# A linear attention and a gated feed-forward on one core: tile 1's first layer as products of quarters, w_in used and summed by column groups, and the loads around it in another order

## The chip, the cores and the metric

The kernel runs on one core of a Trainium2 chip, in one launch. The time is device microseconds of that core. Lower is better.

## The reference, cut to what matters

```python
# batch 8, heads 8, seq 576, head_dim 64;  d_model 512 = 8 x 64, d_ff 2048; all float32
kv  = einsum('bhsd,bhse->bhde', k, v)
out = einsum('bhsd,bhde->bhse', q, kv)
rms = sqrt(mean(out * out, axis=-1, keepdims=True) + 1e-6)
x   = (out / rms * g_norm)            # then (B*S, H*D) = (4608, 512)
h   = x @ w_in                        # (4608, 512) x (512, 2048)
g   = h / (1 + exp(-1.702 * h))       # the gate
y   = g @ w_out                       # (4608, 2048) x (2048, 512)
```

## The kernel before

**Tiles.** The 4608 rows are nine tiles of 512 rows. Tile t (0 to 7) holds 512 of batch t's 576 rows; the last 64 rows of all eight batches make tile 8. For each tile there is a first layer (x times w_in, 16 column blocks of 128, each 4 deep in k) with the gate, and a second layer (the gated values times w_out). Between the instructions of tile t's layers stand those of batch t+1's attention, which makes the x of the next tile. Data are float16 in SBUF (the POOL queue's DMAs convert), sums are float32 in PSUM.

**Dense and seven products.** Tile 0 is dense in both layers (`dense(..., deep=True)`): 64 matmuls of 512 columns each. Tiles 2 to 8 use, in both layers, a form of matrix product that splits both operands into quarters and takes seven products of quarters in place of eight, with sums and differences of quarters as operands (`SevenIn` for the first layer, `Seven` for the second). The first layer is done in four parts of two column blocks in the left half and two in the right. A product is two column blocks times two k blocks: 4 matmuls of 256 columns; a part has seven, a tile 28. It needs four sums of w_in's quarters (`ws`, made once by `w_in_sum`), four sums of x's quarters per tile (`Sums.form`), and for each part: a copy of the first product's bank, a copy of the fifth's to SBUF (`s5`), two additions on VectorE (L544, L546), and four gates on ScalarE. The second layer takes differences of w_out (`tw`, by `weight_sum`) and sums of the gated values (`gS`, by `Seven.sums`). Tile 1 is mixed: its second layer is in seven products, its first is dense (`GROUP` and the ordered first columns in `dense`, then L422).

**The weights' scale.** g_norm is folded into w_in for every tile but the first: batch 0's x is multiplied by it directly, so w_in is scaled in place (`scale_w_in`) only after tile 0's first layer has read it. Before, that is done in tile 0's second layer, whole k blocks at a time: two on ScalarE, two on VectorE.

**What sets the order.** Everything is recorded in program order under a manual schedule; each engine runs its instructions in that order, and semaphores carry the dependencies. `u1` and `u2` hold what is put between the steps: `at1(i, f, ...)` behind step i of a tile's first layer, `at2(n, f, ...)` behind matmul n of its second. For tiles in seven products a `Plan` gives the order by hand: `steps` ("21" is part 2's product 1, "kv" the next batch's k-v product), the places of the sums (`ready`, `later`, `xsums`), the engine of each copy (`snap`: D is VectorE, A is ScalarE), the PSUM pools (a, h, o with 3, 3 and 2 banks), and the places of the attention's steps (`attn`).

**Loads.** They go out on the POOL queue in program order, and a load's issue waits for the landing of an earlier one. The order before is: batch 0's q, k, v by pairs of heads with w_in's first four column blocks between; w_in 4-5, 6-7, 8-9, 10-12, 13-15; w_out 0-3; batch 1's q; w_out 4-7; k of pairs 0-1; w_out 8-9, 10-11; v of pairs 0-1; k, then v of pairs 2-3; w_out 12-13, 14-15; batch 2's q; then batch 2's k and v, each whole. The DMA transposes (q of a batch, and its x) and the stores go out on SyncE's queue.

**PE's order around the change.** Tile 0's first layer takes column blocks 0 to 5 as a group, then 6 to 15 one by one; its second layer has 64 matmuls (L760), between which batch 1's q is transposed (L403), its k-v product made (L221, four pairs), its product with q (L254) and its sums of squares (L329). ACT makes the squares and the roots, DVE multiplies (`apply`), which gives tile 1's x.

Of the kernel before, what the change touches and what calls it, by code (L numbers as in the profile page):

```python
# [16 lines left out]
def kernel(  # L17
# [27 lines left out]
    GROUP = 6  # L45
    assert PE_ * NJ == S and PE_ % 32 == 0
# [59 lines left out]
    def load_kv(b):  # L106
        early_load("k", b, 0, NPAIR)
        early_load("v", b, 0, NPAIR)
# [79 lines left out]
    def scale_w_in(ko, engine):  # L188
        w = w_in_sb[:, ko]
        if engine is nc.scalar:  # L190
            engine.activation(w, w, AFT.Copy, scale=g_col)
        else:
            engine.tensor_scalar_mul(w, w, g_col)
# [198 lines left out]
    class Second(Early):  # L392
# [7 lines left out]
        def q(self, c):  # L400
            t = ps_a.tile([P, S], F16, name="q1", tag="att")
            for j in range(NJ):
                nc.tensor.transpose(  # L403
                    t[:, j * PE_ : (j + 1) * PE_],
                    qbuf[0:PE_, (c * NJ + j) * P : (c * NJ + j + 1) * P],
                    ident[0:PE_, 0:PE_],
                )
# [31 lines left out]
    def w_in_sum(n):  # L439

        a11, a12, a21, a22 = quarters(w_in_sb, slice(0, HF * P), slice(0, KH))
        op, a, b = (
            (nc.vector.tensor_add, a21, a22),
            (nc.vector.tensor_sub, ws[:, 0], a11),
            (nc.vector.tensor_sub, a11, a21),
            (nc.vector.tensor_sub, a12, ws[:, 1]),
        )[n]
        op(ws[:, n], a, b)
# [103 lines left out]
    def weight_sum(n):  # L552
        b11, b12 = w_out_sb[:, 0:HF, 0:HN], w_out_sb[:, 0:HF, HN:DM]
        b21, b22 = w_out_sb[:, HF:FO, 0:HN], w_out_sb[:, HF:FO, HN:DM]
        a, b = ((b12, b11), (b22, tw[:, 0]), (b22, b12), (b21, tw[:, 1]))[n]
        nc.vector.tensor_sub(tw[:, n], a, b)

    class Seven:
# [10 lines left out]
        def sums(self, i0, i1, which=(0, 1, 2, 3)):  # L569
            lo, hi = slice(i0, i1), slice(HF + i0, HF + i1)  # L570
            r1, r2 = slice(0, 2 * P), slice(2 * P, SM)
            g, s = self.gT, self.s
            for n in which:
                op, a, b = (
                    (nc.vector.tensor_add, g[:, lo, r2], g[:, hi, r2]),
                    (nc.vector.tensor_sub, s[:, 0, lo], g[:, lo, r1]),
                    (nc.vector.tensor_sub, g[:, lo, r1], g[:, lo, r2]),
                    (nc.vector.tensor_sub, g[:, hi, r1], s[:, 1, lo]),
                )[n]
                op(s[:, n, lo], a, b)  # L580
# [102 lines left out]
    def hid_seven(t, hid, seven, units1):  # L683


        xs = Sums(t, hid.x)
# [7 lines left out]
        for n, step in enumerate(todo.steps):  # L694
# [12 lines left out]
            for i0, i1, which in todo.ready.get(n, ()):  # L707
                seven.sums(i0, i1, (which,))
# [9 lines left out]
        end = lambda: seven.sums(HF - 2, HF, (0,))  # L718
# [6 lines left out]
    def dense(t, units1, units2, group, deep, hid=None):  # L725
        hid = hid or Hidden(t)
        gT = hid.gT
        seven = None if deep else Seven(t, gT)
        cols = range(FO) if deep else [f for i in range(HF) for f in (i, HF + i)]
        ready = {} if deep else {8: (0, 4), 13: (4, 6), 15: (6, 8, (0,))}  # L730
        if group and t:
            order = [(ko, fo) for part in ((0, 3, 1, 2), range(4, group)) for ko in (0, 1) for fo in part]
            order += [(ko, fo) for ko in range(2, KO) for fo in range(group)]
            for ko, i in order:
                pool = (ps_h, "hT") if i < 3 else (ps_a, "att") if i == 3 else (ps_o, "o")
                hid.mm(ko, cols[i], *pool)
            for i in range(group):
                hid.gate(cols[i])
        left = {}
        if t >= SEVEN:  # L740
            left = hid_seven(t, hid, seven, units1)
            cols = ()
        for i, fo in enumerate(cols):
            if i >= group:
# [3 lines left out]
            for u in units1.get(i, ()):  # L748
                u()
            if i in ready:  # L750
                seven.sums(*ready[i])

        osb = osbs[t] = opool.tile([P, 4, DM], F32, name="osb", tag="osb")
        os = {}

        def project(mo, fo):
# [10 lines left out]
            if fo == FO - 1:  # L767
                copy = nc.scalar.copy if mo % 2 else nc.vector.tensor_copy
                copy(osb[:, mo, :], os[mo])

        if deep:
            steps = [(mo, 4 * i + k) for i in range(3) for mo in range(4) for k in range(4)]
            steps += [(mo, f + k) for f in (12, 14) for mo in range(2) for k in range(2)]
            steps += [(mo, 12 + k) for mo in (2, 3) for k in range(4)]
            for n, (mo, fo) in enumerate(steps):
                project(mo, fo)
                for u in units2.get(n, ()):
                    u()
        else:
            later = plan(t).later if t >= SEVEN else {6: ((6, 8, 1),), 30: ((6, 8, 2), (6, 8, 3))}  # L780
            later = {
                n: [lambda x=x: seven.sums(x[0], x[1], (x[2],)) for x in xs] for n, xs in later.items()
            }
            for n, us in units2.items():
                later.setdefault(n, []).extend(us)
            for n, us in left.items():
                later[n] = us + later.get(n, [])
            seven.run(later)
        if t < EARLY:

            n = 0
            while n < SM:
                mo, j, p = n // P, n // PE_, n % PE_
                m = min((mo + 1) * P, (j + 1) * PE_) - n
                nc.sync.dma_start(
                    out=out[t * S : (t + 1) * S, :][bass.DynSlice(NJ * p + j, m, step=NJ), :],
                    in_=osb[n % P : n % P + m, mo, :],
                )
                n += m
        elif t < B and t not in HALVED:  # L800
            store(t, 0, J)
# [70 lines left out]
    for fo in range(4, GROUP):  # L872
        for ko in range(KO - 1):
            d0.mm(ko, fo, ps_o, "o")
    for fo in range(GROUP):
        d0.mm(KO - 1, fo)
    for fo in range(GROUP):
# [11 lines left out]
    load_w_out(14, FO)  # L889

    osbs = {}
    SEVEN = 2
# [26 lines left out]
    FIRST = {  # L919
        "rows": (1, 7, 14, 20),  # L920
        "add_up": (5, 12, 18, 26),
        "table": 21,
        "roots": (32, 32),
        "turn": (33, 34, 35, 36),
    }

    def plan(t):
        return LATER if t < B - 1 else LAST_TWO
# [7 lines left out]
    for t in range(NT):  # L936
# [12 lines left out]
        if t == 0:  # L949
            at1(7, of(0, "out", NPAIR))  # L950
            at2(4, setattr, a0, "ss_pool", Attention.ss_pool)
            at2(4, of(0, "ss", NPAIR, True))
            at2(4, of(0, "apply", NPAIR))
            at1(8, start, 1)
            at2(5, scale_w_in, 0, nc.scalar)
            at2(6, scale_w_in, 1, nc.scalar)
            at2(33, weight_sum, 0)
            at2(33, scale_w_in, 2, nc.vector)
            at2(34, scale_w_in, 3, nc.vector)
            for n, at in ((2, 35), (0, 39), (1, 40)):  # L960
                at2(at, w_in_sum, n)
            for l in range(2):
                at1(9, nc.vector.memset, kvd[l], 0.0)
            at1(13, load_q, 2)
            for c in range(NPAIR):
                at1(12, of(1, "pack_q", c))
                at2(9 + 3 * c, of(1, "q", c))
                at2((36, 37, 46, 47)[c], of(1, "kv", c))
                o = (41, 43, 52, 53)[c]
                at2(o, of(1, "out", c))  # L970
                if c == NPAIR - 1:
                    at2(48, load_kv, 2)
                at2((45, 48, 56, 58)[c], of(1, "ss", c))
                at2((48, 51, 56, 60)[c], of(1, "apply", c))
        elif b < B:
            if t == 1:
                for n in range(1, 4):
                    at1(0, weight_sum, n)
                at1(9, w_in_sum, 3)
            todo = plan(t) if t >= SEVEN else None  # L980
            at1(todo.steps.index("kv") if todo else 11, of(b, "kv_all", todo.keep if todo else "D"))
            late = 15 if todo else 11
            if t == 1:
                at1(5, start, b)
                at1(5, of(b, "transpose_q"))
            if t + 2 < B:
                at1(late, load_kv, t + 2)
# [3 lines left out]
            at = todo.attn if todo else FIRST  # L991
# [18 lines left out]
        dense(t, u1, u2, (GROUP, 5)[t] if t < 2 else 0, t == 0, None if t else d0)  # L1010
# [30 lines left out]
```

## Time and profile before

| what | value |
|---|---|
| median of 3 runs | 264.03 us (263.69 to 264.33) |
| profiled execution: its own time | 263.92 us |
| its span, first to last instruction | 262.1 us |
| granted TensorE clock, mean | 0.996 |
| busy: PE, PEld (weight loads), DVE, ACT, POOL | 253.6, 204.3, 185.1, 173.6, 43.7 us |
| tile 0's first layer, most of it | 16.42 to 28.97 us |
| tile 0's second layer with batch 1's attention | 28.97 to 47.31 us |
| tile 1's first layer | 47.31 to 62.11 us |
| tile 1's second layer | 62.11 to 75.46 us |

Times in the chain of waits are those of the links, which for a run of matmuls begin 0.16 us behind the start of its first one: a matmul of 256 columns is shown with 273 ns, but the next one ends 0.11 us later. In the timeline and in the table of groups the durations are those of single instructions, which on DVE and ACT overlap a little with the next one.

### The profile page before, as it was taken

The numbers are of one execution on the slowest core, as the hardware profiler recorded it, in microseconds if no ns is written. First come the engines' busy times: TensorE is split into PE (matmuls) and PEld (weight loads), VectorE is DVE, ScalarE is ACT, GpSimd is POOL, SyncE is SP. The second block draws the span as 40 slices with busy tenths as digits, with TensorE's granted clock in tenths as the row PEclk, the third lists the DMA queues.
The fourth block names the chain that finished last, engine by engine and source line by source line (L and its number), as shares of the span: only waits on it lengthen the run. The fifth ranks groups of instructions, "written<-read, shape, count | busy, mean of one in ns | idle before, by whom it ended". The sixth has DMA issues, their size and how long they took to land.

```text
span 262.1 us, 6210 instructions
## 1 busy us (share of the span) xinstructions
PE 253.6 (97%) x2556; PEld 204.3 (78%) x2556; DVE 185.1 (71%) x324; ACT 173.6 (66%) x308; POOL 43.7 (17%) x68
## 2 busy tenths in 40 slices
PE   6899999999999999999999999999999999999992
PEld 5434554447888988898889988998899888888882
DVE  1540378868768995899589958995899587567831
ACT  3459836776649963996489748974798469737810
POOL 8863242005005001400050005000000000000000
PEclk9999999999999999999999999999999999999998
DMA  7999999999989946996899769946600620021005
GB/s 173 197 199 205 205 203 177 217 206 130 163 180 172 221 58 160 117 240 83 145 154 196 102 157 150 237 54 154 165 0 8 156 83 0 3 100 63 0 3 160
DMA packets 59806, 35.32 MB, mean 135 GB/s; under 512 B 31554, under 2 KB 57154, under 8 KB 59650
## 3 DMA queue, kind: packets, MB, share of 16 engines
q0 software_dynamic: 28608, 18.17, 50.1%
q1 hardware_dynamic: 30768, 16.36, 27.1%
q8 instruction: 20, 0.33, 0.5%
q10 hardware_dynamic: 402, 0.39, 0.5%
q14 instruction: 8, 0.07, 0.1%
HBM read 36.70 MB, written 9.44 MB: 176 GB/s over the span
## 4 chain that ended last, share of the span: by engine, by line
PE 92%; DMA 4%; POOL 1%; DVE 0%; issue 0%; ACT 0%; ACTq 0%
PE o L648 37%; PE h L530 33%; PE hT L422 10%; PE o L760 5%; PE kvp L221 2%; DMA vbuf<-in_v_dram 2%; DMA qraw<-in_q_dram 2%; PE outR L281 2%; PE ss L329 1%; PE outT L254 0%; PE q L403 0%; PE outT L258 0%; POOL kraw L89 0%; ACT sq L272 0%; DVE osb L628 0%
## 5 line engine op out<-in xcount | busy, mean ns | idle before, releaser
L648 PEld LDWEIGHTS <-gS 128*128 128x128 f16 x512 | 49.8, 98 | 5.5
L510 ACT ACTIVATE gT<-h 128x512 f16<-128x512 f32 x84 | 46.2, 605 | 5.1 <-PE h L530 5.1
L530 PEld LDWEIGHTS <-ws 128*128 128x128 f16 x448 | 43.8, 98 | 5.1
L648 PE MATMUL o<-tw,gS 128*128 128x256 f16 x384 | 46.3, 273 | 0.0
L530 PE MATMUL h<-xS,ws 128*128 128x256 f16 x336 | 45.3, 273 | 0.0
L648 PEld LDWEIGHTS <-gT 128*128 128x128 f16 x384 | 37.1, 98 | 4.2
L530 PEld LDWEIGHTS <-w_in_sb 128*128 128x128 f16 x336 | 32.5, 98 | 3.9
L648 PE MATMUL o<-w_out_sb,gT 128*128 128x256 f16 x256 | 33.3, 273 | 0.0
L422 PE MATMUL hT<-xT,w_in_sb 128*128 128x512 f16 x128 | 28.9, 379 | 0.0
L625 DVE TENSOR_TENSOR osb<-o,qf 128x512 f32<-128x512 f32 (+1 forms) x25 | 16.7, 668 | 15.6 <-PE o L648 12.8
L530 PE MATMUL h<-xT,w_in_sb 128*128 128x256 f16 x192 | 27.1, 273 | 0.0
L89 POOL DMA_DIRECT2D kraw<-in_k_dram x11 | 8.1, 733 | 106.3 <-PE kvp L221 87.8
L580 DVE TENSOR_TENSOR gS<-gT 128x512 f16<-128x512 f16 (+2 forms) x34 | 22.0, 653 | 4.5 <-ACT gT L431 3.9
L544 DVE TENSOR_TENSOR h<-h,s 128x512 f32<-128x512 f32 x28 | 19.5, 698 | 7.4 <-PE h L530 5.6
L422 PEld LDWEIGHTS <-w_in_sb 128*128 128x128 f16 x128 | 12.3, 98 | 15.4 <-issue 0.9
L431 ACT ACTIVATE gT<-hT 128x512 f16<-128x512 f32 x32 | 17.6, 613 | 7.0 <-PE hT L422 7.0
L546 DVE TENSOR_TENSOR s<-h,s 128x512 f32<-128x512 f32 x28 | 19.4, 692 | 4.0 <-PE h L530 3.3
L331 ACT ACTIVATE rs<-ss,eps_t 128x512 f32<-128x512 f32 (+1 forms) x16 | 9.2, 584 | 16.4 <-PE ss L329 16.3
L510 ACT ACTIVATE gT<-s 128x512 f16<-128x512 f32 x28 | 17.3, 628 | 1.2 <-DVE s L546 1.2
L944 ACT ACT_TABLE_LOAD x14 | 18.0, 1283 | 0.3
L681 POOL DMA_DIRECT2D out_dram<-osb x2 | 1.1, 562 | 94.1 <-DVE osb L625 94.1
L760 PE MATMUL o<-w_out_sb,gT 128*128 128x512 f16 x64 | 16.7, 380 | 0.0
(93 smaller groups left out, 367.6 us busy)
## 6 DMA issues: line engine op xcount, KB each, us to landing
out_dram<-osb SPq DMA_DIRECT2D x10, 512.0 KB, 3.5
kraw<-in_k_dram POOLq DMA_DIRECT2D x6, 576.0 KB, 8.7
vbuf<-in_v_dram POOLq DMA_DIRECT2D x6, 576.0 KB, 12.1
qraw<-in_q_dram POOLq DMA_DIRECT2D x3, 512.0 KB, 13.3
qbuf<-in_q_dram POOLq DMA_DIRECT2D x3, 512.0 KB, 14.0
out_dram<-osb SPq DMA_DIRECT2D x6, 192.0 KB, 6.9
w_in_sb<-in_moe_w_in_dram POOLq DMA_DIRECT2D x4, 256.0 KB, 7.5
w_out_sb<-in_moe_w_out_dram POOLq DMA_DIRECT2D x2, 512.0 KB, 14.0
```

Source lines behind the costliest of these rows:

```text
L331: nc.scalar.activation(rs[:, 0:n], t[:, 0:n], AFT.Abs_reciprocal_sqrt, bias=eps_t, scale=1.0 / D)
L422: nc.tensor.matmul(self.h[fo], w_in_sb[:, ko, fo * P : (fo + 1) * P], self.x[:, ko], start=(ko == 0), stop=(ko == KO - 1),)
L431: nc.scalar.activation(self.gT[:, fo, :], self.h[fo], AFT.Gelu_apprx_sigmoid)
L510: nc.scalar.activation(self.gT[:, to, n * TH : (n + 1) * TH], src, AFT.Gelu_apprx_sigmoid)
L530: nc.tensor.matmul(bank[name][:, a], w, x, start=(p in (1, 5) and a == 0 and k == 0), stop=(k == KH - 1), skip_group_check=True,)
L544: nc.vector.tensor_add(bank["z"], bank["x"], self.s5)
L546: nc.vector.tensor_add(self.s5, bank["x"], self.s5)
L580: op(s[:, n, lo], a, b)
L625: nc.vector.tensor_add(o, ps, self.kept[with_][:, m])
L648: nc.tensor.matmul(o, a, w, start=(p in (1, 2, 5) and i == 0 and (mo == 0 or split)), stop=(i == HF - 1), skip_group_check=True,)
L760: nc.tensor.matmul(os[mo], gT[:, fo, mo * P : (mo + 1) * P], w_out_sb[:, fo, :], start=(fo == 0), stop=(fo == FO - 1),)
L944: u2.setdefault(i, []).append(lambda: f(*args))
```

## The change

Five things are done together.

1. Tile 1's first layer becomes 28 products of quarters by a new `Plan`, `SECOND`. Tile 1's x lies as (c, n), so `Sums` takes it without the regrouping; the first sum of x is formed behind step 55 of tile 0's second layer.
2. w_in's column blocks are used by tile 0 in the order `COLS` and loaded in the order 0-3, 8-9, 10-11, 4-7, 12-15. `scale_w_in` and the sums of w_in work on groups of columns (0-3 with 8-11, 4-5 with 12-13, 6-7 with 14-15), all on VectorE: the first two groups between the columns of tile 0's first layer, the third in its second layer.
3. The differences of w_out are made in pieces: in tile 0's second layer, the last three (for blocks 6-7) in tile 1's first.
4. w_out 12-13 is loaded ahead of batch 1's k and v of pairs 2-3; the k-v products of these pairs and what follows from them stand one to three steps later in tile 0's second layer.
5. Batch 2's k and v are loaded in halves, behind steps 39 and 51 of that layer; the copies of batch 1's transposed q out of PSUM go from VectorE to ScalarE.

The function `dense` is split into `layers`, `first_columns`, `project_all` and `store_early`, with no other effect on the order.

```diff
+    COLS = (0, 1, 2, 3, 8, 9, 10, 11, 4, 5, 12, 13, 6, 7, 14, 15)
...
-    load_w_in(4, GROUP)
-    load_w_in(GROUP, 8)
     load_w_in(8, 10)
-    load_w_in(10, 13)
-    load_w_in(13, FO)
+    load_w_in(10, 12)
+    load_w_in(4, 8)
+    load_w_in(12, FO)
...
-    def scale_w_in(ko, engine):
-        w = w_in_sb[:, ko]
-        if engine is nc.scalar:
-            engine.activation(w, w, AFT.Copy, scale=g_col)
-        else:
-            engine.tensor_scalar_mul(w, w, g_col)
+    def scale_w_in(i0, i1):
+
+        for i in (i0, HF + i0):
+            w = w_in_sb[:, :, i * P : (i + i1 - i0) * P]
+            nc.vector.tensor_scalar_mul(w, w, g_col)
...
-            nc.vector.tensor_copy(s, t)
+            nc.scalar.copy(s, t)
             self.qT[c] = s
...
+    def w_in_sums(g0, g1):
+
+        f = slice(2 * g0 * P, 2 * g1 * P)
+        a11, a12, a21, a22 = quarters(w_in_sb, f, slice(0, KH))
+        s = [ws[:, n, :, f] for n in range(4)]
+        nc.vector.tensor_add(s[0], a21, a22)
+        nc.vector.tensor_sub(s[1], s[0], a11)
+        nc.vector.tensor_sub(s[2], a11, a21)
+        nc.vector.tensor_sub(s[3], a12, s[1])
...
-            x = x if t < B else x.rearrange("p c (j r) -> p c j r", j=J)
+            x = x if EARLY <= t < B else x.rearrange("p c (j r) -> p c j r", j=J)
...
-    def weight_sum(n):
...
+    def weight_sum(n, i0, i1):
+
+        lo, hi = slice(i0, i1), slice(HF + i0, HF + i1)
...
     early_load("v", 1, 0, 2)
+    load_w_out(12, 14)
     early_load("k", 1, 2, NPAIR)
     early_load("v", 1, 2, NPAIR)
-    load_w_out(12, 14)
     load_w_out(14, FO)
...
+    SECOND = Plan(
+        "01 15 11 05 02 06 21 16 12 07 25 03 26 22 04"
+        " 35 31 27 13 17 36 kv 32 24 23 14 37 33",
+        {24: ((0, 4, 0),), 26: ((0, 4, 1),), 27: ((4, 6, 0),)},
+        {0: ((0, 4, 3),), 4: ((0, 8, 2),), 26: ((4, 8, 1),), 72: ((4, 8, 3),)},
+        {1: 'AAAA', 5: 'DADD'},
+        "D",
+        "aoaa",
+        "ahoh",
+        {5: '34'},
+        (-1, 0, 0, 4),
+        {'rows': (0, 2, 8, 19), 'add_up': (6, 26, 27, 31), 'table': 26, 'roots': (27, 33), 'turn': (40, 50, 51, 52)},
+    )
...
         if t == 0:
+            for l in range(2):
+                at1(6, nc.vector.memset, kvd[l], 0.0)
             at1(7, of(0, "out", NPAIR))
+            at1(7, scale_w_in, 0, 4)
+            at1(7, w_in_sums, 0, 2)
+            at1(8, start, 1)
+            at1(11, scale_w_in, 4, 6)
+            at1(11, w_in_sums, 2, 3)
+            at1(13, load_q, 2)
...
+            at2(18, weight_sum, 0, 0, HF)
+            at2(18, scale_w_in, 6, 8)
+            at2(18, w_in_sums, 3, 4)
             for c in range(NPAIR):
                 at1(12, of(1, "pack_q", c))
                 at2(9 + 3 * c, of(1, "q", c))
-                at2((36, 37, 46, 47)[c], of(1, "kv", c))
-                o = (41, 43, 52, 53)[c]
...
+                at2((36, 37, 49, 50)[c], of(1, "kv", c))
+                at2((41, 43, 54, 55)[c], of(1, "out", c))
+                at2((45, 50, 58, 60)[c], of(1, "ss", c))
+                at2((48, 52, 58, 62)[c], of(1, "apply", c))
+            for n in range(1, 4):
+                at2(19, weight_sum, n, 0, 4)
+                at2(38, weight_sum, n, 4, 6)
+            at2(39, load_kv, 2, 0, 2)
+            at2(51, load_kv, 2, 2, NPAIR)
+
+            def first_sum():
+                made[1] = Sums(1, xT[1])
+                made[1].form(0)
+
+            at2(55, first_sum)
...
             if t == 1:
                 at1(5, start, b)
                 at1(5, of(b, "transpose_q"))
+                at1(4, nc.scalar.preload_act_table_set, "gelu_apprx_sigmoid_and_others")
+                for n, i in ((1, 8), (2, 11), (3, 16)):
+                    at1(i, weight_sum, n, 6, HF)
```

More of the change, by code (lines that the diff above doesn't have):

```diff
@@ L567, in __init__, with sums @@
             self.bank, self.kept = {}, None
-        def sums(self, i0, i1, which=(0, 1, 2, 3)):
+        def sums(self, i0, i1, *which):
             lo, hi = slice(i0, i1), slice(HF + i0, HF + i1)
@@ L707, in hid_seven @@
             for i0, i1, which in todo.ready.get(n, ()):
-                seven.sums(i0, i1, (which,))
+                seven.sums(i0, i1, which)
         for u in gates:
@@ L723, in hid_seven, with layers, first_columns @@
         return left
[L725 to L744, printed above, removed]
+    def layers(t, units1, units2):
+        hid = d0 if t == 0 else Hidden(t)
+        seven = Seven(t, hid.gT) if t else None
+        left = hid_seven(t, hid, seven, units1) if t else first_columns(hid, units1)
+        osbs[t] = opool.tile([P, 4, DM], F32, name="osb", tag="osb")
+        if t:
+            todo = {n: [lambda x=x: seven.sums(*x) for x in xs] for n, xs in plan(t).later.items()}
+            for n, us in units2.items():
+                todo.setdefault(n, []).extend(us)
+            for n, us in left.items():
+                todo[n] = us + todo.get(n, [])
+            seven.run(todo)
+        else:
+            project_all(hid.gT, units2)
+        if t < EARLY:
+            store_early(t)
+        elif t < B and t not in HALVED:
+            store(t, 0, J)
+    def first_columns(hid, units):
+        for i, fo in enumerate(COLS):
+            if i >= GROUP:
                 for ko in range(KO):
@@ L747, in dense, with project_all @@
                 hid.gate(fo)
-            for u in units1.get(i, ()):
+            for u in units.get(i, ()):
                 u()
-            if i in ready:
-                seven.sums(*ready[i])
-        osb = osbs[t] = opool.tile([P, 4, DM], F32, name="osb", tag="osb")
+    def project_all(gT, units):
         os = {}
@@ L768, in project, with store_early @@
                 copy = nc.scalar.copy if mo % 2 else nc.vector.tensor_copy
[L769 to L801, printed above, removed]
+                copy(osbs[0][:, mo, :], os[mo])
+        steps = [(mo, 4 * i + k) for i in range(3) for mo in range(4) for k in range(4)]
+        steps += [(mo, f + k) for f in (12, 14) for mo in range(2) for k in range(2)]
+        steps += [(mo, 12 + k) for mo in (2, 3) for k in range(4)]
+        for n, (mo, fo) in enumerate(steps):
+            project(mo, fo)
+            for u in units.get(n, ()):
+                u()
+    def store_early(t):
+        n = 0
+        while n < SM:
+            mo, j, p = n // P, n // PE_, n % PE_
+            m = min((mo + 1) * P, (j + 1) * PE_) - n
+            nc.sync.dma_start(
+                out=out[t * S : (t + 1) * S, :][bass.DynSlice(NJ * p + j, m, step=NJ), :],
+                in_=osbs[t][n % P : n % P + m, mo, :],
+            )
+            n += m
     def store(t, j0, j1):
@@ L967 @@
                 at2(9 + 3 * c, of(1, "q", c))
-                at2((36, 37, 46, 47)[c], of(1, "kv", c))
-                o = (41, 43, 52, 53)[c]
[L970 to L974, printed above, removed]
-        elif b < B:
[L976 to L982, printed above, removed]
+                at2((36, 37, 49, 50)[c], of(1, "kv", c))
[11 more added lines that the diff above has]
+            at2(55, first_sum)
+        elif b < B:
+            todo = plan(t)
+            at1(todo.steps.index("kv"), of(b, "kv_all", todo.keep))
             if t == 1:
```

61 lines of the change are left out of this document (18 added, 43 removed).

## The prediction

> **What bounds the kernel now.** I read the page first, then the chain of waits in order of time, then PE's own waits.
>
> ```profile
> span 262.1 us, 6210 instructions
> PE 253.6 (97%) x2556; PEld 204.3 (78%) x2556; DVE 185.1 (71%) x324; ACT 173.6 (66%) x308; POOL 43.7 (17%) x68
> PE 92%; DMA 4%; POOL 1%; DVE 0%; issue 0%; ACT 0%; ACTq 0%
> 22.06 6.91 PE hT L422 x32
> ...
> 31.24 0.26 PE q L403 x6
> ...
> 38.10 0.31 PE kvp L221 x12
> ...
> 41.74 0.31 PE kvp L221 x12
> ...
> 47.31 10.36 PE hT L422 x48
> 57.67 0.88 PE kvp L221 x48
> 58.55 3.56 PE hT L422 x16
> ...
> 77.21 11.02 PE h L530 x100
> ...
> PE idle L831 <- DVE one_t L176: 1.3, 1, 1.3
> ...
> PE outT L254 <- DVE kvb L373: 0.4, 1, 0.4
> ```
>
> The chain is PE for 92% of the span, and tile 1's first layer (47.31 to 62.11 us, with batch 2's k-v product inside) is one unbroken run of PE on it. All of PE's waits (five rows, first and last shown) belong to instructions of batch 0's start. So from tile 0 on TensorE is the limit: each PE microsecond that goes away is worth one, and each wait that is put in costs one. The profiled execution took 263.92 us (span 262.1, 1.8 around it); the median of the three runs is 264.03, and I carry differences over to that median. A change of 0.2%, 0.53 us, is about what a measurement of this kernel can tell.
>
> **1. What the products remove from PE.** Tile 1's dense layer is 64 matmuls 512 wide: 10.36 + 3.56 = 13.92 us (0.2175 each). The new one is 28 products of 4 matmuls 256 wide. 11.02/100 = 0.110 us each, so 112 cost 12.34 (0.441 a product). Removed: **1.58 us**. Batch 2's k-v product (0.88) stays. The sum rests on a 256-wide matmul costing half a 512-wide one, which the rows show, 0.110 against 0.2175. The Trainium skill speaks against this (TensorE: Matmul & The Clock Gate, Back-to-back issue gap): in a stream of weight load and matmul pairs it gives about 131 ns for 512 columns and 81 for 128. By it an estimate between the two, 98 ns for 256, would make the layer 11.0 us against 8.4, a loss of 2.6. The trace does not agree; its 216 to 218 ns decide.
>
> **2. w_in in another order: a new wait in tile 0.** POOL's issues wait for earlier loads, so their starts date the landings.
>
> ```profile
> 16.38 0.76 POOL L180 DMA_DIRECT2D w_out_sb<-in_moe_w_out_dram  x1 [0.25 <-DMA w_in_sb<-in_moe_w_in_dram]
> ...
> 19.00 0.70 POOL L180 DMA_DIRECT2D w_out_sb<-in_moe_w_out_dram  x1 [0.35 <-DMA w_in_sb<-in_moe_w_in_dram]
> 20.33 0.72 POOL L180 DMA_DIRECT2D w_out_sb<-in_moe_w_out_dram  x1 [0.62 <-DMA w_in_sb<-in_moe_w_in_dram]
> 22.61 0.69 POOL L89 DMA_DIRECT2D vbuf<-in_v_dram  x1 [1.57 <-DMA w_in_sb<-in_moe_w_in_dram]
> 24.53 0.67 POOL L89 DMA_DIRECT2D kraw<-in_k_dram  x1 [1.23 <-DMA w_in_sb<-in_moe_w_in_dram]
> ...
> 29.76 0.71 POOL L180 DMA_DIRECT2D w_out_sb<-in_moe_w_out_dram  x1 [2.02 <-DMA qraw<-in_q_dram]
> 32.37 0.70 POOL L180 DMA_DIRECT2D w_out_sb<-in_moe_w_out_dram  x1 [1.90 <-DMA w_out_sb<-in_moe_w_out_dram]
> ```
> ```profile
> 29.50 1.39 DVE L96 COPY qbuf<-qraw 96x768 f16<-96x768 f16 x4 [10.49 <-DMA qraw<-in_q_dram]
> ```
>
> Batch 1's q is seen by DVE at 29.50 and by POOL at 29.76, so a landing is some 0.26 before POOL's start. w_in's pieces to column 8, 10, 13 and 16 thus landed at 18.74, 20.07, 22.35 and 24.27. The new pieces are the same bytes: columns 8-9 and 10-11 by 18.7, 4-7 by about 21.4, and 12-15, now one 512 KB load, complete at 23.9 to 24.3. The columns run 0.864 us each from 22.06 (6.91/8). Before, the eleventh was column 10, long there, and columns 13 to 15 came last. Now the eleventh is column 12: due at 22.06 + 2x0.864 = 23.79, its weight load about 0.25 before (a row's start lies 0.16 ahead of its link in the chain, and a load leads its matmul by 0.1): 23.55. PE waits **0.4 us** (between 0, if the bigger piece arrives faster, and 0.8). Columns 4-7 are due at 21.8 and cost nothing, with 0.4 to spare.
>
> **3. DVE's scaling and sums under tile 0's first layer.** DVE is idle there for 10.49 us.
>
> ```profile
> L193 DVE TENSOR_SCALAR w_in_sb<-w_in_sb,g_col 128x2048 f16<-128x2048 f16 x2 | 1.4, 746 | 0.0
> L580 DVE TENSOR_TENSOR gS<-gS,gT 128x1024 f16<-128x1024 f16 x15 | 10.4, 692 | 0.5
> L580 DVE TENSOR_TENSOR gS<-gT 128x512 f16<-128x512 f16 x18 | 7.4, 418 | 0.9 <-ACT gT L431 0.9
> 35.05 0.64 POOL L122 DMA_DIRECT2D qrem<-in_q_dram  x1
> 36.32 0.99 POOL L122 DMA_DIRECT2D qrem<-in_q_dram  x1 [0.64 <-DMA w_out_sb<-in_moe_w_out_dram]
> 35.76 1.41 DVE L193 TENSOR_SCALAR w_in_sb<-w_in_sb,g_col 128x2048 f16<-128x2048 f16 x2
> ```
>
> The first group starts when column 11 is done (22.0): two scalings 1.4, four sums of 0.69; the second waits for column 13 (26.0 with the wait above): two scalings of about 0.4, four sums of 0.42. DVE is through at 28.5, one us before it must pack batch 1's q at 29.50. Cost 0; were the cover gone, the first transpose of q (31.24 in the chain) would move one for one. Later DVE gets two waits on loads: w_out's first differences for columns 4-7 (32.37 - 0.26 = 32.1), the next three for w_out 10-11 (36.1). Queued behind them are the third group's scalings and sums (done by 36) and batch 1's k-v casts, due at about 39; DVE is through the three at 38.1: 0. ACT loses two scalings and takes four q copies into its idle time after 31 us: 0. On POOL, an issue that overlapped the scalings took 0.99 against 0.64, and in the new order two scalings lie over the issue of batch 1's first v. That agrees with the Trainium skill (SBUF — State Buffer, "DVE blocks DMA" trap): a two-port DVE operation locks GpSimd out of writing descriptors. That v was issued at 22.61 and is used at 38.10, so a few tenths are hidden.
>
> **4. The loads of batch 1 and 2.**
>
> ```profile
> 53.39 3.08 SPq L244 DMA_TRANSPOSE qTd<-qraw  x1
> ...
> qTd<-qraw SPq DMA_TRANSPOSE x1, 4.9
> ```
>
> w_out 12-13 go ahead of batch 1's last k and v. From w_out 10-11 (36.32 - 0.26 = 36.1) the 288 + 256 + 288 + 288 KB to the last v take 5.7 us at 512 KB per 2.62 (16.38 to 19.00): 41.8. It was used at 41.74 by the chain, and now three projections later: 41.74 + 0.65 - 0.16 = 42.2, plus part 2's wait. w_out 14-15 keep their place. Cost 0 (to 0.3). Batch 2's halves add two issues on POOL, ahead of nothing that PE uses before 56 us. The transposes of batch 2's q wait on SP for the last v of batch 2, whose bytes end the same queue: issued at 53.4, landed 4.9 later at 58.3, used from 60.1 on: 0.
>
> **5. Tile 1's first layer: DVE and ACT behind PE.** Here the change adds most: a tile's four x sums, eight additions, and eight copies out of PSUM (five on ACT).
>
> ```profile
> 47.30:62.10 14.80, 14.80 (x115) 7.06 (x113) 11.44 (x18) 10.10 (x17) 3.25 (x5) 1.00 0.96 180
> 75.30:88.20 12.90, 12.90 (x160) 11.45 (x158) 10.61 (x20) 10.42 (x21) 3.68 (x5) 1.00 1.00 191
> ```
> ```profile
> L544 DVE TENSOR_TENSOR h<-h,s 128x512 f32<-128x512 f32 x28 | 19.5, 698 | 7.4 <-PE h L530 5.6
> L480 DVE CAST kvd<-kvp 64x256 f16<-64x256 f32 x24 | 10.1, 420 | 0.3
> 54.89 0.69 DVE L580 TENSOR_TENSOR gS<-gT 128x1024 f16<-128x1024 f16 x1 [3.03 <-ACT gT L431]
> 55.61 0.69 DVE L580 TENSOR_TENSOR gS<-gS,gT 128x1024 f16<-128x1024 f16 x1
> 56.23 0.68 DVE L580 TENSOR_TENSOR gS<-gT 128x1024 f16<-128x1024 f16 x1
> 44.39 1.08 ACT L272 ACTIVATE sq<-outT 128x512 f16<-128x512 f32 x2 [0.45 <-PE outT L254]
> 45.83 1.29 ACT L331 ACTIVATE rs<-ss,eps_t 128x512 f32<-128x512 f32 x2
> 68.23 2.48 DVE L309 TENSOR_TENSOR x<-outR,sum 128x512 f16<-128x512 f32 x4 [0.75 <-ACT sum L305]
> ```
>
> I laid the new order on DVE and ACT beside PE's. A DVE operation lets the next start 0.62 after it (0.72 where that one reads it; 55.61 and 56.23), 0.34 for half a one. The third root ends 0.22 later than before (its product stands a projection later): 45.83 + 0.69 + 0.22 = 46.74, so two applies and an output copy end at 48.7, two x sums at 49.5, a copy and the last x sum follow, and the first addition runs 50.37 to 51.06. The tenth product reads behind it and is due at 47.15 (47.31 less the 0.16) + 9x0.441 = 51.12: with the hand-over it waits **0.1**. After the k-v product DVE has four casts, six sums and an addition up to 63.57; the last of these is due at 63.8. ACT reaches the gate that frees layer 2's bank at 60.0, due 59.94: **0.1**. Batch 1's last sum of squares now has an output copy between the two squares ahead of it on ACT: **0.1**. Together 0.3; bounds 0 and 0.8, since DVE has no slack: eight additions (5.5), three copies (2.0), six half-size sums (2.5), four casts (1.7), two applies and an output copy (2.1) are 13.8 us of operations in a stage of 13.2. ACT and DVE come out of the stage earlier than before, batch 2's scaled rows are done at 69.1 by the same tally against 68.23 + 2.48 = 70.7, so tile 2 starts on time. All later tiles are unchanged: 0.
>
> **Sum**: -1.58 + 0.4 + 0 + 0 + 0.3 = -0.88. I take **-0.8**, since the bounds reach further up than down: 263.1 for the profiled execution, **263.2** for the median.
>
> **Rivals.**
> - *All hidden*: the last w_in piece lands in time and DVE keeps up. For it: both margins are tenths. Against it: POOL's rows date the bytes at 24.27 and column 12 at 23.55. 264.03 - 1.58 = 262.4 (262.2 to 262.8).
> - *The saving is eaten*: waits at their upper bounds, 0.8 + 0.3 + 0.8 = 1.9 against 1.58. For it: parts 2 and 5 each have a place without slack. 264.0 to 264.4.
> - *Slower: DVE becomes the bound in tile 1.* If its 30 operations from the third apply to the last sum run one after the other at the dependent pace, 0.1 more each, they end 3.0 later; 0.2 of that is covered, then layer 2 waits for its sums. With w_in's 0.4 and ACT's two waits: -1.58 + 0.4 + 0.2 + 2.8 = +1.8, 265.8. It makes the kernel slower from 1.7 us of lengthening on. For it: stage 47.30 to 62.10 had DVE 11.44 busy with three large sums that nobody waited for, and gets more. Against it: the steady stage (75.30 to 88.20) does the same products with 10.61 in 12.9 without a PE wait.
> - *256-wide matmuls dearer than half* (the change saves nothing): it needs over 13.92/112 = 0.124 us each; the 100 in a row show 0.110. No chance.
>
> **How the numbers follow.** Forecast 0.38, all hidden 0.22, eaten 0.21, DVE-bound 0.19. The first two are faster by over 0.2%, the third counts as the same, the fourth as slower. The range, 262.4 to 264.6, leaves out the better half of the second case and most of the fourth.
>
> **What would show it.** In the profile after: L422 with half its 128 matmuls, 112 more on L530; tile 1's first layer 13.2 us with the k-v product; a PE wait of about 0.4 on w_in in tile 0 near 23.6, small ones near 51 (on DVE) and 60 (on ACT). I am wrong on part 2 if PE shows no wait on w_in, on part 5 if the stage is over 14 us or layer 2 waits for the sums of the gated tile, and in the whole if PE's waits after 16 us come to over 1.6.

## The result, and the profile after

| | before | after |
|---|---|---|
| median of 6 runs each, us | 263.75 (263.61 to 264.33) | 262.73 (262.49 to 263.09) |
| ratio, 95% interval | | 0.9958 (0.9945 to 0.9971) |
| profiled execution, us | 263.92 | 262.49 |
| its span, us | 262.1 | 260.7 |

The change saves 1.02 us of the medians, 0.4%. The forecast was 263.2 from 264.03, a saving of 0.8.

The page after, its first lines and the chain by engine:

```profile
span 260.7 us, 6349 instructions
PE 252.9 (97%) x2604; PEld 209.1 (80%) x2604; DVE 194.2 (74%) x349; ACT 174.4 (67%) x315; POOL 44.2 (17%) x69
...
PE 89%; DMA 6%; POOL 2%; issue 0%; DVE 0%
```

PE is still the chain. Its busy time fell by 0.7 us only; a short wait between matmuls counts as busy there (the row of 7.38 us below holds one of 0.31), so the gain is read from starts along the chain. The chain of waits after, in order of time (start, us, what):

```profile
12.55 11.30 DMA w_in_sb<-in_moe_w_in_dram
...
23.90 5.35 PE hT L421 x24
...
47.75 9.21 PE h L528 x84
56.97 0.88 PE kvp L220 x48
57.84 2.73 PE h L528 x24
...
76.12 11.02 PE h L528 x100
...
256.38 0.42 DVE osb L628
```

Tile 1's layer is now L528, in 84 + 24 matmuls (the last four of the 112 stand behind layer 2's first ones), where before stood 48 + 16 on L422. Tile 2's run of 100 starts at 76.12; before, at 77.21. So the gain, 1.09, is complete at tile 2, and the links from there on are the same ones, to 0.07 in all. At the end the last addition on DVE starts at 256.38, where before had it here:

```profile
257.41 0.42 DVE osb L628
```

That is 1.03 earlier. The spans differ by 1.4; the other 0.4 lies behind this addition, in the last store, which the change doesn't touch. The medians differ by 1.02, as the chain does.

The list of PE's waits names none of the new ones. All its five rows are of batch 0's start, as before; the sum of squares in the last one is batch 0's (first line of the timeline below), which waited before too.

```profile
PE ss L328 <- ACT sq L271: 0.2, 1, 0.2
```

PE's timeline shows the new ones (start, us, line, tiles, count; a row joins matmuls that follow each other, so a short wait is inside a row):

```profile
13.07 0.38 PE L328 MATMUL ss<-sq,ones 128*128 128x512 f16 x1 [0.23 <-ACT sq L271]
...
21.88 7.38 PE L421 MATMUL hT<-xT,w_in_sb 128*128 128x512 f16 x32
...
46.14 0.59 PE L762 MATMUL o<-w_out_sb,gT 128*128 128x512 f16 x2
46.73 0.38 PE L328 MATMUL ss<-sq,ones 128*128 128x512 f16 x1
...
47.59 0.60 PE L528 MATMUL h<-xT,w_in_sb 128*128 128x256 f16 x4
...
51.08 0.60 PE L528 MATMUL h<-xT,w_in_sb 128*128 128x256 f16 x4
51.57 1.03 PE L528 MATMUL h<-xS,ws 128*128 128x256 f16 x8
...
60.41 0.27 PE L648 MATMUL o<-w_out_sb,gT 128*128 128x256 f16 x1
```

The row at 21.88 holds the 32 matmuls of tile 0's last eight column blocks, the ninth (block 4) to the last. They took 7.07 in one piece where w_in was there (experiment e3, below): 7.38 holds a wait of 0.31, the one on w_in's last load, and the chain's first two rows here name it, ending at 23.85. The sum of squares at 46.73 was due at 46.14 + 2 x 0.216 = 46.57: 0.16. The product at 51.57 was due 0.437 after 51.08: 0.05. ACT's and DVE's timelines show what each of the two waited for:

```profile
45.60 0.58 ACT L771 COPY osb<-o 128x512 f32<-128x512 f32 x1
46.06 0.62 ACT L271 ACTIVATE sq<-outT 128x512 f16<-128x512 f32 x1
```
```profile
50.82 1.29 DVE L542 TENSOR_TENSOR h<-h,s 128x512 f32<-128x512 f32 x2
```

The square that the sum needs stands behind an output copy and ends at 46.68. The first of the two additions (0.69) ends at 51.51. Layer 2's first product, at 60.41, follows the last of layer 1 at its pace: no wait.

### The profile page after: what moved, and what is told of

Same layout as the page of the kernel before. It is cut to its first block, busy times and chain, and to the rows that moved or that the text cites. A ratio compares the mean times of both kernels' runs of the same rounds, so it can differ in the third digit from the quotient of the medians.

```text
span 260.7 us, 6349 instructions
## 1 busy us (share of the span) xinstructions
PE 252.9 (97%) x2604; PEld 209.1 (80%) x2604; DVE 194.2 (74%) x349; ACT 174.4 (67%) x315; POOL 44.2 (17%) x69
## 3 DMA queue, kind: packets, MB, share of 16 engines
q1 hardware_dynamic: 30768, 16.36, 27.9%
## 4 chain that ended last, share of the span: by engine, by line
PE 89%; DMA 6%; POOL 2%; issue 0%; DVE 0%
PE h L528 38%; PE o L648 38%; PE o L762 5%; DMA w_in_sb<-in_moe_w_in_dram 4%; PE kvp L220 2%; DMA qraw<-in_q_dram 2%; PE outR L280 2%; PE hT L421 2%; POOL w_in_sb L154 1%; PE ss L328 1%; PE q L402 0%; PE outT L253 0%; PE outT L257 0%; POOL kraw L90 0%; POOL vbuf L90 0%
## 5 line engine op out<-in xcount | busy, mean ns | idle before, releaser
L508 ACT ACTIVATE gT<-h 128x512 f16<-128x512 f32 x96 | 52.8, 604 | 5.4 <-PE h L528 5.3
L528 PEld LDWEIGHTS <-ws 128*128 128x128 f16 x512 | 50.1, 98 | 5.9
L528 PE MATMUL h<-xS,ws 128*128 128x256 f16 x384 | 52.2, 273 | 0.0
L528 PEld LDWEIGHTS <-w_in_sb 128*128 128x128 f16 x384 | 37.1, 98 | 4.7
L528 PE MATMUL h<-xT,w_in_sb 128*128 128x256 f16 x224 | 31.9, 273 | 0.0
L544 DVE TENSOR_TENSOR s<-h,s 128x512 f32<-128x512 f32 x32 | 22.1, 691 | 3.9 <-PE h L528 3.1
L528 PE MATMUL h<-xS,w_in_sb 128*128 128x256 f16 x128 | 18.9, 273 | 0.0
L478 ACT COPY h<-h 128x512 f32<-128x512 f32 x27 | 15.6, 585 | 2.1 <-PE h L528 2.0
L478 ACT COPY s<-h 128x512 f32<-128x512 f32 x18 | 10.6, 588 | 9.5 <-PE h L528 8.8
L528 PE MATMUL h<-xT,ws 128*128 128x256 f16 x112 | 16.8, 273 | 0.0
```

Source lines behind the costliest of these rows:

```text
L478: (nc.vector.tensor_copy if engine == "D" else nc.scalar.copy)(to, src)
L508: nc.scalar.activation(self.gT[:, to, n * TH : (n + 1) * TH], src, AFT.Gelu_apprx_sigmoid)
L528: nc.tensor.matmul(bank[name][:, a], w, x, start=(p in (1, 5) and a == 0 and k == 0), stop=(k == KH - 1), skip_group_check=True,)
L544: nc.vector.tensor_add(self.s5, bank["x"], self.s5)
```

## The experiments

Theory A is the prediction's account: PE is the limit throughout, the products take 1.58 us off it, and what comes back is small waits, one on w_in, two on ScalarE and one on VectorE, each worth its length. The rivals of each run stand with its expectation. Ratios are to the kernel before, run on the same chip.

**e1: the changed kernel with tile 1's first layer dense again.** The column order, the sums of w_in and the loads around tile 0 stay; the places of the attention's steps and of the gated sums in tile 1 are those of the kernel before, which the lines below do not show.

```
-        left = hid_seven(t, hid, seven, units1) if t else first_columns(hid, units1)
+        if t == 1:
+            left = first_dense(hid, seven, units1)   # the loop of before
+        else:
+            left = hid_seven(t, hid, seven, units1) if t else first_columns(hid, units1)
```

> The changed kernel with tile 1's first layer dense again (64 matmuls 512 wide, the attention's places and the gated sums of the kernel before); the new w_in order, the sums by column groups, the loads and the copies on ScalarE stay. Theory A (what was taken off PE is the gain): the first layer takes 14.8 us with the k-v product instead of 13.2, tile 2 starts 1.5 us later than in the changed kernel, and the whole is 1.4 to 1.6 slower than it and 0.3 to 0.5 slower than the kernel before (the w_in wait and the wait of the last sum of squares stay): 264.1 to 264.3. Theory B (the gain comes from the order of loads and sums, not from the products): it stays within 0.5 us of the changed kernel, 262.7 to 263.2.

264.28 against 264.15: 1.0024 (1.0000 to 1.0048). The chain of waits of this kernel:

```profile
46.98 0.38 PE ss L328
...
48.00 10.36 PE hT L421 x48
58.36 0.88 PE kvp L220 x48
59.24 3.56 PE hT L421 x16
...
77.90 11.02 PE h L528 x100
```

From the layer's first link to tile 2's run it is 77.90 - 48.00 = 29.90; in the changed kernel 76.12 - 47.75 = 28.37. The products save 1.53, and the whole gain goes with them: what else the change does brings nothing by itself. The dense layer runs without a gap here (10.36 + 0.88 + 3.56 = 14.80, as before), so the difference is PE's own work and not the attention's places. The wait ahead of the last sum of squares is here too (0.38 for a link of 0.21), so it belongs to the new order of batch 1's steps and not to the products.

**e2: the kernel before with the column order and the load order alone.**

```
+    COLS = (0, 1, 2, 3, 8, 9, 10, 11, 4, 5, 12, 13, 6, 7, 14, 15)
-    load_w_in(4, GROUP)
-    load_w_in(GROUP, 8)
     load_w_in(8, 10)
-    load_w_in(10, 13)
-    load_w_in(13, FO)
+    load_w_in(10, 12)
+    load_w_in(4, 8)
+    load_w_in(12, FO)
-        cols = range(FO) if deep else [f for i in range(HF) for f in (i, HF + i)]
+        cols = COLS if deep else [f for i in range(HF) for f in (i, HF + i)]
```

> The kernel before with one part of the change: tile 0 uses w_in's column blocks in the new order and they are loaded in the new order, the last four as one load. Everything else, the scaling in tile 0's second layer too, is as before. Theory A (the eleventh column waits for the last load): PE waits 0.3 us on w_in near 23.6 us, and all that follows is 0.3 later: 0.1 to 0.15% slower, below what can be told from times alone, but plain in the chain of waits, and tile 1's first layer starts at 47.6 instead of 47.31. Theory B (the wait in the changed kernel comes from VectorE's scaling delaying the issue of loads): no wait on w_in here, 47.3.

264.19 against 264.15: 0.9998 (0.9984 to 1.0012). Its PE and POOL timelines:

```profile
21.99 7.35 PE L422 MATMUL hT<-xT,w_in_sb 128*128 128x512 f16 x32
```
```profile
21.92 0.69 POOL L90 DMA_DIRECT2D vbuf<-in_v_dram  x1 [2.11 <-DMA w_in_sb<-in_moe_w_in_dram]
```

The wait is 7.35 - 7.07 = 0.28 with nothing on DVE at that time, so it comes of the loads and their order, not of the early scaling. Its 0.3 lies within the interval of the ratio; the trace shows it, the times alone would not.

**e3: the changed kernel with w_in's last load in two.**

```
-    load_w_in(12, FO)
+    load_w_in(12, 14)
+    load_w_in(14, FO)
```

> The changed kernel with w_in's last load (column blocks 12 to 15) split in two, 12-13 and 14-15. Theory A (the eleventh column, block 12, waits for the end of a 512 KB load whose first half is there 1.3 us earlier): blocks 12-13 land at about 22.8, PE's wait of 0.3 us near 23.6 is gone, tile 1 starts 0.3 earlier, total about 0.3 lower: 262.4. Theory B (the halves arrive together, or smaller pieces are slower): the wait stays and the time is 262.7 or more.

262.63 against 264.15: 0.9934 (0.9909 to 0.9960). PE's timeline:

```profile
22.24 7.07 PE L422 MATMUL hT<-xT,w_in_sb 128*128 128x512 f16 x32
```

The wait is gone. The bytes and their order are the same; column 12 needed only the first half of them and had waited for the whole 512 KB. This run's columns began 0.4 us later than the changed kernel's (22.24 against 21.88), so the loads had some more time; e6 has the same split with an early start. The total forecast, 262.4, was not reached, and 262.63 lies between the two theories' times: the trace decides here, the time does not.

**e4, e7, e8: the copies out of PSUM, moved between VectorE and ScalarE.** Tile 1's plan gives five of its eight copies to ACT. One string says which.

```
 {1: 'AAAA', 5: 'DADD'}   the changed kernel
 {1: 'DDDD', 5: 'DDDD'}   e4: all on VectorE
 {1: 'AAAA', 5: 'DDDD'}   e7: one more on VectorE
 {1: 'AAAA', 5: 'AAAA'}   e8: all on ScalarE
```

> The changed kernel with the five copies out of PSUM in tile 1's first layer that ScalarE makes put on VectorE (all eight there): 5 x 0.62 = 3.1 us more for VectorE in a stage in which it idled 0.25 us, 2.4 us less for ScalarE. Theory A (VectorE has no slack there, the rival on the slower side): PE waits inside tile 1's layers for 2.3 to 2.8 us, and the total is 265.0 to 265.5. Theory B (the additions and sums have margin enough, as in the steady tiles): PE's waits grow by less than 0.5 us, 262.7 to 263.2.

264.96 against 264.15: 1.0028 (1.0008 to 1.0048). PE's timeline now has DVE's name on it:

```profile
50.28 0.60 PE L528 MATMUL h<-xT,w_in_sb 128*128 128x256 f16 x4 [0.33 <-DVE h L478]
...
53.68 1.03 PE L528 MATMUL h<-xS,ws 128*128 128x256 f16 x8 [0.50 <-DVE h L542]
```

From the layer's first product to layer 2's it is 62.73 - 48.04 = 14.69, against 60.41 - 47.59 = 12.82: 1.87 more, which undoes the whole gain. Up to tile 2 it is 78.74 - 48.04 = 30.70 against 76.12 - 47.59 = 28.53, 2.17 more, a little under the 2.3 to 2.8 of theory A. DVE bounds tile 1 here, as in the prediction's slower rival, but by five more copies; that rival's own reason, a slower pace of the operations, did not occur (a copy on DVE lets the next start after 0.60 here).

> The changed kernel with one copy more on VectorE in tile 1's first layer (part 1's fifth product; 0.62 us more of VectorE, 0.48 less of ScalarE). Theory A (VectorE has no slack from the third apply to the first addition): the first addition comes 0.6 later, product 7 of part 0 waits 0.6 instead of 0.05, and the total is 0.5 to 0.6 above the changed kernel. Theory B (the slow run with all eight copies on VectorE was due to the four copies that the next product waits for, not to VectorE's load): 0 to 0.2.

263.30 against 264.17: 0.9965 (0.9944 to 0.9985). One copy on DVE instead of ACT:

```profile
52.53 1.03 PE L528 MATMUL h<-xS,ws 128*128 128x256 f16 x8 [0.48 <-DVE h L542]
```

The same product that waits 0.05 in the changed kernel is held up by DVE here, and the layer takes 61.37 - 47.96 = 13.41, 0.59 more than 12.82. A copy is 0.6 us of work, so all of it shows: DVE has nothing to spare there. The median is 0.63 above e5's, the changed kernel on the same chip.

> The changed kernel with all eight copies of tile 1's first layer on ScalarE: VectorE has 3 x 0.62 = 1.9 us less, ScalarE 3 x 0.48 = 1.4 more. Theory A (VectorE alone is short of slack): the wait of 0.05 us at product 7 goes away and nothing comes in its place; equal to the changed kernel within 0.1 us. Theory B (ScalarE is as full: it idled 2 us in that stage and its gates free the banks): the copies push the gates, PE waits for banks near the end of the first layer or for the first row products, 0.3 to 1.0 slower.

263.39 against 264.17: 0.9962 (0.9936 to 0.9987). The other way, with three copies moved, the layer takes 61.09 - 47.74 = 13.35, 0.53 more, and the median is 0.72 above e5's. The product behind the first addition does not wait now, but the chain of waits runs through ScalarE, which no row of before or after has in this layer:

```profile
47.90 3.94 PE h L528 x36
51.85 0.60 ACT gT L508
...
56.51 0.50 ACT h L478
```

ACT's timeline has no gap from 47.94 to 58.5, and PE's waits lie inside that stretch (0.11, 0.26 and 0.21 by the starts of its products). ACT's idle time comes behind it:

```profile
59.17 2.07 ACT L508 ACTIVATE gT<-h 128x512 f16<-128x512 f32 x4 [0.62 <-PE h L528]
```

The windows of the layer (13.2 us from about its start; busy us of PE, PEld, DVE, ACT, POOL, each with its count, then granted clock, DMA share and GB/s) for the changed kernel, for e4 and for e8:

```profile
47.30:60.50 13.20, 13.20 (x160) 11.52 (x158) 12.65 (x25) 11.84 (x21) 2.35 (x3) 1.00 0.90 181
```
```profile
48.00:61.20 13.20, 11.92 (x143) 9.92 (x142) 13.19 (x26) 7.16 (x13) 0.73 (x1) 1.00 0.87 172
```
```profile
47.50:60.70 13.20, 13.05 (x155) 11.06 (x154) 10.72 (x21) 12.51 (x24) 1.86 (x3) 1.00 0.96 181
```

In the changed kernel DVE is busy 12.65 of 13.2 and ACT 11.84, and PE is held up by 0.05 only. Full DVE (13.19) leaves PE 11.92. In e8 ACT has 0.7 us idle in the sum and still holds PE up, since nearly all of it lies behind the stretch in which PE waits; a share of busy time does not tell where the idle time lies.

**e5 and e6: the changed kernel again, and with both waits taken out.** e5 is the changed kernel itself, on the chip of e6, e7 and e8. e6 splits the last load as e3 does and lets the last sum of squares stand one projection later:

```
-    load_w_in(12, FO)
+    load_w_in(12, 14)
+    load_w_in(14, FO)
-                at2((45, 50, 58, 60)[c], of(1, "ss", c))
+                at2((45, 50, 58, 61)[c], of(1, "ss", c))
```

> The changed kernel itself, once more, as the measure for the three beside it on the same chip. Both theories: 0.4% below the kernel before; the wait on w_in's last load is between 0 and 0.3 us, according to how late tile 0's first column starts on this chip (0.28 where it started at 16.4 us, none in the runs that started at 16.9).

> The changed kernel with w_in's last load in two halves (as in the run before) and batch 1's last sum of squares one projection later, behind step 61 of tile 0's second layer, so that ScalarE's square for it is ready. Theory A (PE is the bound, and every wait taken out is gained): PE's run from tile 0's first column to tile 1's start is 0.15 us shorter by the sum of squares, and up to 0.3 by the load; total 0.15 to 0.45 below the changed kernel, and no wait on PE but those of batch 0's start and under 0.1 near 51 us. Theory B (the roots and the applies behind the later sum become late in its place): the wait reappears in tile 1's first products behind an apply or an x sum, and the time is that of the changed kernel.

e5: 262.67 against 264.17, 0.9936 (0.9912 to 0.9961). PE's timeline:

```profile
22.23 7.36 PE L421 MATMUL hT<-xT,w_in_sb 128*128 128x512 f16 x32
```

Its wait on w_in is 7.36 - 7.07 = 0.29, though this row began 0.35 later than in the first profile. A later start does not take the wait away, as I had expected it to: e1 and e4, whose rows began at 22.20 and 22.44 against 21.88, kept 0.2. The loads move with the start, wholly or in part.

e6: 262.41 against 264.17, 0.9931 (0.9908 to 0.9954). PE's timeline:

```profile
21.82 7.07 PE L422 MATMUL hT<-xT,w_in_sb 128*128 128x512 f16 x32
```
```profile
47.06 0.60 PE L529 MATMUL h<-xT,w_in_sb 128*128 128x256 f16 x4
...
48.05 0.60 PE L529 MATMUL h<-xT,w_in_sb 128*128 128x256 f16 x4
...
60.03 0.27 PE L649 MATMUL o<-w_out_sb,gT 128*128 128x256 f16 x1
```
```profile
47.42 0.58 ACT L772 COPY osb<-o 128x512 f32<-128x512 f32 x1
```

The start is as early as in the changed kernel (21.82 and 21.88), and no wait on w_in is left, so the split removes it without help from a later start. Both waits out should bring 0.47. From the start of the last eight column blocks to layer 2 it is 60.03 - 21.82 = 38.21 against 60.41 - 21.88 = 38.53, 0.32 less; the layer itself takes 12.97 instead of 12.82. The 0.15 of the sum of squares came back: 0.11 at the third product (48.05, due at 47.06 + 2 x 0.437 = 47.94), which takes a bank of the pool that tile 0's outputs used and starts when an output copy on ACT ends (48.00), and the rest at the product behind the first addition. PE's first product came 0.53 earlier than in the changed kernel (47.06 against 47.59), DVE's third apply only 0.38 (46.91 against 47.29), the roots on ACT 0.37 (46.18 against 46.55). So theory A holds for two thirds of what was taken out, theory B for the rest. The medians of e6 and e5 differ by 0.26. It is the fastest version run, though its interval overlaps the changed kernel's.

**e9: the loads of w_out 12-13 and of batch 2's k and v as before.**

```
-    load_w_out(12, 14)
     ...
+    load_w_out(12, 14)
-            at2(39, load_kv, 2, 0, 2)
-            at2(51, load_kv, 2, 2, NPAIR)
+            at2(51, load_kv, 2)
```

> The changed kernel with the loads of batches 1 and 2 as before: w_out 12-13 behind batch 1's last k and v, batch 2's k and v whole behind step 51; the places of the products stay. Theory A (the prediction's part 4: these moves cost and bring nothing as long as each piece lands before its product): no PE wait beside the changed kernel's in tile 0's second layer, the transposes of batch 2's q go out within 0.5 us of the changed kernel's, and the time is equal within 0.2 us. Theory B (w_out 12-13, landing about 42.1 in this order, is now late for its product, which stands at 41.9 to 42.3 since the k-v products were moved behind it): PE waits 0.2 to 0.7 us on w_out near 42, and the total is as much higher.

262.81 against 264.25: 0.9941 (0.9925 to 0.9958), which can't be told from the changed kernel. Its trace can: PE's timeline and PE's waits have

```profile
57.48 0.95 PE L220 MATMUL kvp<-vbuf,kraw 96*64 96x64 f16 x48 [0.37 <-DMA vbuf<-in_v_dram]
```

Batch 2's k-v product waits 0.4 for v, and the layer takes 61.00 - 47.74 = 13.26 instead of 12.82. So the halves are worth 0.4 in one profile, though the median does not show it: the products bring the k-v product forward (56.97 against 57.67), and one whole load behind the last k-v product of batch 1 no longer lands ahead of it. Neither theory had this wait. The transposes of batch 2's q go out at 53.60, 2.7 later than in the changed kernel, and not within the 0.5 that theory A gave. The order of w_out 12-13 costs PE nothing, against theory B: from 42 to 47 no wait of over 0.05 appeared or went. On DVE it shows, since the differences of w_out 12-13 wait for the load (they start at 39.98 in the changed kernel):

```profile
42.21 0.43 DVE L556 TENSOR_TENSOR tw<-w_out_sb,tw 128x512 f16<-128x512 f16 x1 [2.14 <-DMA w_out_sb<-in_moe_w_out_dram]
```

**e10: the q copies back on VectorE.**

```
-            nc.scalar.copy(s, t)
+            nc.vector.tensor_copy(s, t)
```

> The changed kernel with the four copies of batch 1's transposed q back on VectorE (4 x 0.46 us between 31 and 35 us). Theory A (VectorE has room there: the first w_out difference waits for a load until 32.1 and the sums are needed only in tile 1): no PE wait, equal within 0.2 us. Theory B (the copies stand ahead of the third group's scalings and sums and of the w_out differences, and push batch 1's k-v casts): a PE wait before batch 1's first product with q near 40, 0.2 to 0.8 us slower.

263.03 against 264.25: 0.9964 (0.9940 to 0.9987), which overlaps the changed kernel's interval. Its profiled execution began batch 0 late, with a granted clock of 0.985 on the mean, so only distances behind it are read. DVE's and PE's timelines:

```profile
40.48 0.45 DVE L408 COPY qT<-q 128x576 f16<-128x576 f16 x1
...
42.65 0.58 DVE L356 CAST kvb<-kvp 64x128 f16<-64x128 f32 x2
```
```profile
42.22 1.04 PE L762 MATMUL o<-w_out_sb,gT 128*128 128x512 f16 x4
43.29 0.39 PE L253 MATMUL outT<-qT,kvb 128*128 128x512 f16 x1
```

The last q copy stands ahead of w_out's three differences on DVE, and these ahead of batch 1's k-v casts; `outT` starts 1.07 after the four projections' start, where the changed kernel has 40.13 - 39.25 = 0.88. By this one trace, the copies' move to ACT is worth 0.2.

## Why the prediction was right, point by point

**PE bounds the kernel; the products take 1.58 off it.** Right: e1 has 1.53. The 84 matmuls in a row took 9.21, 0.110 each, as the steady tiles had. The Trainium skill's paced figures (TensorE: Matmul & The Clock Gate, Back-to-back issue gap), by which I had estimated a loss here, do not hold for this stream: it goes at 110 ns for 256 columns and 216 for 512.

**The wait on w_in: 0.4 forecast, 0.31 measured** (0.2 to 0.3 over the runs with the whole load, 0 in e3 and e6). The place, the column and the cause were right; the landing, put at 23.9 to 24.3 from POOL's starts, was at 23.85. The size was 0.1 too high, which is no more than the runs differ among themselves.

**DVE's sums under tile 0's first layer: 0.** Right. DVE and POOL after:

```profile
21.96 0.75 DVE L192 TENSOR_SCALAR w_in_sb<-w_in_sb,g_col 128x2048 f16<-128x2048 f16 x1 [1.40 <-PE hT L421]
...
27.50 0.42 DVE L446 TENSOR_TENSOR ws<-w_in_sb,ws 128x512 f16<-128x512 f16 x1
29.50 1.36 DVE L97 COPY qbuf<-qraw 96x768 f16<-96x768 f16 x4 [1.59 <-DMA qraw<-in_q_dram]
```
```profile
21.80 1.16 POOL L90 DMA_DIRECT2D vbuf<-in_v_dram  x1 [2.10 <-DMA w_in_sb<-in_moe_w_in_dram]
```

The sums end at 27.9 (forecast 28.5; one of the first group's two scalings had already run at 19.80, and not with the other at 22) and q is packed from 29.50 as before, on its load. Batch 1's first v took 1.16 to issue where e2, without the scaling, had 0.69: 0.47 more, hidden as forecast, though one scaling lay over it and not two. ScalarE's four q copies were put down at 0 too; e10 shows that in the changed order they would have cost 0.2 on DVE, so the move was part of what keeps this part at 0, which I had not seen.

**The loads: 0.** Right in sum, but partly by luck. I took batch 2's halves for two more issues that nobody waits for; by e9 they cover 0.4 us that the earlier k-v product would have waited. I had not seen that wait; the change happened to hold what takes it away. The transposes of batch 2's q were forecast at 53.4 as before and came earlier, with the halves:

```profile
50.90 3.85 SPq L243 DMA_TRANSPOSE qTd<-qraw  x1
```

**Tile 1's layer: 0.3 forecast, 0.2 measured.** For the sum of squares 0.1 was forecast and 0.16 measured, for the product behind the first addition 0.1 and 0.05, for layer 2's bank 0.1 and 0. The tally of DVE and ACT beside PE held to 0.1 us in all three places. It had to be that fine for DVE, which has nothing to give ahead of the first addition (e7); ACT has a little more, as three copies, some 1.5 us, cost 0.53 there (e8). Batch 2's scaled rows were done at 67.02 + 2.48 = 69.50, forecast 69.1, and tile 2 started on time.

**The sum.** -1.58 + 0.31 + 0.16 + 0.05 = -1.06, against -1.02 by the medians and -1.09 by the chain at tile 2. Forecast terms gave -0.88, and I took -0.8 for the bounds above. That last step was the weakest: three of the four terms of waits were 0.05 to 0.1 too high, one 0.06 too low, and I moved the sum further up.

**The rivals.** All hidden: not so, as 0.5 us of waits exist (e6 came within 0.2 of it by its trace). Eaten: no term came near its upper bound. DVE-bound: not reached, but next door: one copy more on DVE costs its whole length (e7), five cost 1.9 (e4).

## What to carry to other kernels

When one engine runs without a gap, fewer instructions on it are worth their paced time, and the risk is in what the faster stage now meets early: the engines that feed it and the loads that were just in time. Lay the helpers' operations out in order beside the bound engine at the pace that the rows show; where their slack is a tenth, one operation more costs its whole length. Here a consumer waited for the whole of a load whose first half was all it needed, so the load that ends last ahead of its use is the one to split.

## What had not been expected of the hardware

ScalarE with 0.7 us idle in a stage of 13.2 held PE up by 0.53 (e8), nearly as much as one copy too many on VectorE (0.59, e7): a busy share does not show where the idle time lies. Of the waits removed on PE a third came back within 2 us, most of it behind ScalarE (e6: 0.47 taken out, 0.32 kept). And a DMA issue on GpSimd grew from 0.69 (e2; 0.69 in e6 too, where it stands behind the scaling) to 1.16 us under a VectorE scaling of 0.75. This agrees with the Trainium skill (SBUF — State Buffer, "DVE blocks DMA" trap). The transfer was not wanted for 16 us, and nothing came of it.
